# An attention and expert kernel whose row loads keep their place in SyncE's queue

## The chip, the cores and the metric

The kernel runs on one core of a Trainium2 chip. Its engines are TensorE (PE; its weight loads are listed as PEld), VectorE (DVE), ScalarE (ACT), GpSimd (POOL) and SyncE (SP), which here only issues DMAs. Each engine has a queue of its own that it works through in order. The metric is the device time of one execution in microseconds (us).

## What is computed

Causal attention with a decay over 4 batches, 8 heads, 576 positions and 64 columns a head; then a gated feed-forward layer (512 to 2048 to 512); then a soft mixture of 8 experts with 4 slots each. All in float32 in the reference:

```python
scores = scale * np.matmul(q, k.transpose(0, 1, 3, 2))
cum = np.cumsum(np.log(np.clip(f, 0.0001, 1.0)), axis=-1)
scores = np.where(causal, -1e9, scores + cum[..., :, None] - cum[..., None, :])
attn = softmax(scores)                      # over the last axis
x = np.matmul(attn, v)                      # -> (2304, 512)
h = x @ w_in
x = (h * (1.0 / (1.0 + np.exp(-1.702 * h)))) @ w_out
logits = x @ phi                            # 32 slots
slot_input = softmax(logits over tokens).T @ x
slot_out[e] = np.maximum(slot_input[e] @ w1[e], 0.0) @ w2[e]   # 8 experts
return softmax(logits over slots) @ slot_out
```

## The kernel before

The attention is cut into 20 rows, numbered 0 to 19: 4 batches of 5 blocks of positions (four of 128, one of 64). A row needs its queries and the keys and values of the rows of its batch up to itself. To keep precision with float16 matmuls, keys, queries and values are split into a high and a low float16 part.

For each row, `load_row` (lines 274 to 293) issues loads of keys, queries and values from DRAM on SyncE (line 290) into the tiles kf, qf and vf, of which there is one buffer each. `prep_row` (295 to 346) then makes the operands of the score matmuls: ScalarE casts the keys (line 300, kbn) and the queries (303, qbn), VectorE copies them beside the decay terms (304, 305 and 310: kan, qan) and subtracts to get the low parts (307, 311; on GpSimd for rows 1 to 4). The four tiles kan, qan, kbn and qbn, one buffer each, are transposed: for rows 0 to 2 on TensorE, from row 3 on by four DMA transposes on SyncE (line 328), traced in the order kan, qan, kbn, qbn. Their outputs qa and qb have two buffers each, those of the keys (kab) six. Values are split on ScalarE and VectorE (334, 335). At its end `prep_row` of row r calls `load_row` of row r + 1, so the loads of a row are traced right after the last transpose of the row ahead.

Rows 0 to 4 use a form in which the row maxima are found first (`emit_max`, line 369, tile mt). Rows 5 to 19 use `emit_qk`: score matmuls (533, 534; 545 and 548 for the short rows), the row's exponentials on ScalarE (560), a split into pn (568, 569) and a DMA transpose of pn to ph on SyncE (573), of which ph has three buffers; then the matmuls with the values (610 to 612) read ph.

Beside the attention runs the feed-forward layer (`moe_steps`, lines 754 to 779: matmuls hp, 762 to 764), in 9 pieces of 256 tokens, and ahead of it the conversion of its weights (lines 203 to 262: tiles raw, low, w, wo), which come as 32 loads of 512 KB on SyncE. Attention and feed-forward steps are traced interleaved. After both, 128 loads of 256 KB bring the expert weights.

What order the instructions get is not that of the trace: the tile framework sorts each engine's queue on a simulated time line when the kernel is built, and lets an instruction pass another on its engine where no data or buffer stands against it. `tc.keep_in_program_order(x)` adds one edge, from the instruction traced last on x's engine to x, so that x cannot be sorted ahead of that one. In the kernel before it is used for the first key cast and for some filler matmuls.

Of the kernel before, what the change touches and what calls it, by code (L numbers as in the profile page):

```python
# [30 lines left out]
def attention_moe_softmoe(ctx, tc, q, k, v, f, w_in, w_out, phi, w1, w2, out):  # L31
    nc = tc.nc
# [93 lines left out]
    def setup_decay():  # L126
        fs = ap_.tile([BH, S], F32, tag="kab2", name="fs")
        nc.sync.dma_start(out=fs, in_=f.rearrange("b h s -> (b h) s"))

        nc.gpsimd.memset(nmst, 1.0)  # L130
        nc.scalar.activation(out=nmst, in_=nmst, func=AF.Ln)
        ones = ap_.tile([BH, S], F32, tag="kab3", name="ones")
        nc.vector.memset(ones, 1.0)
        cum = ap_.tile([BH, 128 * NQ], F32, tag="kab4", name="cum")
        nc.vector.memset(cum[:, S:], 0.0)
        load_row(0, "kq")
        nc.vector.tensor_scalar(
            out=fs, in0=fs, scalar1=1e-4, scalar2=1.0, op0=ALU.max, op1=ALU.min
        )
        nc.scalar.activation(out=fs, in_=fs, func=AF.Ln)  # L140
        r = ap_.tile([128, NQ, BH], F32, tag="dg", name="cres")
        nc.scalar.activation(out=r[0:BH, 0, 0:1], in_=fs[:, 0:1], func=AF.Exp)
        nc.vector.tensor_tensor_scan(
            out=cum[:, 0:S], data0=ones, data1=fs, initial=0.0, op0=ALU.mult, op1=ALU.add
        )
        pt = ps_mi("cumT")
        ct = pt[:, 0:NQ * BH].rearrange("p (i c) -> p i c", i=NQ)
        for i in range(NQ):
            nc.tensor.transpose(ct[:, i, :], cum[:, 128 * i:128 * (i + 1)], ident[0:BH, 0:BH])
        nc.vector.tensor_scalar(out=r, in0=ct, scalar1=-1.0 / SC, scalar2=None, op0=ALU.mult)  # L150
        for j in range(3):
            nc.vector.tensor_copy(cpart[:, :, :, j], r)
            if j < 2:
                nc.vector.tensor_tensor(out=r, in0=r, in1=cpart[:, :, :, j], op=ALU.subtract)
# [119 lines left out]
    def load_row(r, names="kqv"):  # L274
        b, i = rows[r]
        n = rows_of[i]
        for nm in names:
            if nm == "v" and b in B32:
                VV[r] = t = ap_.tile([128, H, D + 1], F32, tag="vv", name="vv", bufs=6)
                nc.gpsimd.memset(t[0:n, :, D:D + 1], 1.0 / VS)  # L280
                t = t[:, :, 0:D]
            elif r < 3:

                if r not in first_kq:
                    first_kq[r] = wp.tile([128, 2, 512], F32, tag=f"o{7 - r}", name="kqf")
                t = first_kq[r][:, nm == "q"].rearrange("p (h d) -> p h d", h=H)
            else:
                t = ap_.tile([128, H, D], F32, tag=nm + "f", name=nm + "f", bufs=1)
            src = {"q": q, "k": k, "v": v}[nm]
            nc.sync.dma_start(  # L290
                out=t[0:n], in_=src[b, :, 128 * i:128 * i + n, :].rearrange("h p d -> p h d")
            )
            nat[r, nm + "f"] = t

    def prep_row(r):
# [46 lines left out]
        if r == 0:  # L342
            load_row(0, "v")
            load_row(1, "v")
        elif r + 1 < len(rows):
            load_row(r + 1)
# [875 lines left out]
```

## Time and profile before

| | |
|---|---|
| median of 3 runs | 600.77 us (592.6 to 602.49) |
| profiled execution | 600.44 us |
| its span, first to last instruction | 598.7 us |
| busy: PE, DVE, ACT, POOL | 531.8, 357.7, 311.0, 69.8 us |
| mean granted TensorE clock | 0.938 of full speed |
| row loads (keys, queries, values) | 256 KB each (128 KB for the short rows), about 4 us to landing |

All times of the profile are from one execution and count from its first instruction. A busy engine need not be the one that sets the time; a wait is listed as "who waited, for whom". A DMA's own line shows how long SyncE took to issue it, not when its data landed.

### The profile page before, as it was taken

The numbers are of one execution on the slowest core, as the hardware profiler recorded it, in microseconds if no ns is written. First come the engines' busy times: TensorE is split into PE (matmuls) and PEld (weight loads), VectorE is DVE, ScalarE is ACT, GpSimd is POOL, SyncE is SP. The second block draws the span as 40 slices with busy tenths as digits, with TensorE's granted clock in tenths as the row PEclk, the third lists the DMA queues.
The fourth block names the chain that finished last, engine by engine and source line by source line (L and its number), as shares of the span: only waits on it lengthen the run. The fifth ranks groups of instructions, "written<-read, shape, count | busy, mean of one in ns | idle before, by whom it ended". The sixth has DMA issues, their size and how long they took to land.

```text
span 598.7 us, 13680 instructions
## 1 busy us (share of the span) xinstructions
PE 531.8 (89%) x5399; PEld 337.0 (56%) x5399; DVE 357.7 (60%) x956; ACT 311.0 (52%) x602; POOL 69.8 (12%) x120
## 2 busy tenths in 40 slices
PE   4484899999989999999989989989999989899992
PEld 4473668867756656655556555565665544374331
DVE  8978769646765476695585666785653332320242
ACT  6756577647765465665566655765542332201122
POOL 4866443310000000000000000000000000000000
PEclk9677699989998999999999999998997999869997
DMA  9996494959994374999964799954551399929988
GB/s 250 265 346 159 96 203 144 213 106 176 170 179 76 54 134 79 177 162 167 149 102 92 129 165 190 159 74 90 79 78 24 116 371 384 338 92 338 380 282 267
DMA packets 229823, 105.63 MB, mean 176 GB/s; under 512 B 202592, under 2 KB 211296, under 8 KB 229760
## 3 DMA queue, kind: packets, MB, share of 16 engines
q1 hardware_dynamic: 227296, 102.41, 74.9%
q10 hardware_dynamic: 2464, 2.36, 1.2%
q8 instruction: 42, 0.69, 0.5%
q14 instruction: 21, 0.17, 0.1%
HBM read 64.63 MB, written 4.72 MB: 116 GB/s over the span
## 4 chain that ended last, share of the span: by engine, by line
PE 67%; DMA 11%; DVE 7%; ACT 6%; issue 3%; POOL 2%; SPq 1%; ACTq 1%; POOLq 0%; DVEq 0%
PE hp L762 9%; PE hp L763 8%; PE hp L764 8%; PE gT L738 5%; DMA kf<-in_k_dram 3%; DMA ph<-pn 3%; PE p L742 3%; PE pv L605 3%; PE sp L862 3%; PE pv L610 3%; PE l L1102 3%; DMA qb<-qbn 2%; PE so L1125 2%; PE wps L252 2%; PE scs L533 2%
## 5 line engine op out<-in xcount | busy, mean ns | idle before, releaser
L762 PE MATMUL hp<-w,xt 128*128 128x512 f16 x288 | 111.0, 385 | 0.0
L763 PE MATMUL hp<-w,xt 128*128 128x512 f16 x288 | 110.5, 384 | 0.0
L764 PE MATMUL hp<-w,xt 128*128 128x512 f16 x288 | 110.1, 382 | 0.0
L560 ACT ACTIVATE pf<-scs,mx 128x512 f32<-128x512 f32 (+3 forms) x108 | 58.1, 544 | 39.9 <-DVE mx L556 32.7
L771 DVE SCALAR_TENSOR_TENSOR g<-g,hp 128x512 f32<-128x512 f32 x72 | 49.2, 683 | 45.5 <-ACT g L770 45.4
L770 ACT ACTIVATE g<-hp 128x512 f32<-128x512 f32 x72 | 42.6, 592 | 62.0 <-PE hp L764 61.7
L569 DVE SCALAR_TENSOR_TENSOR pn<-pf,pn 128x512 f16<-128x512 f32 (+2 forms) x78 | 51.1, 657 | 27.7 <-ACT pn L568 26.7
L568 ACT ACTIVATE pn<-pf 128x512 f16<-128x512 f32 (+2 forms) x78 | 47.2, 608 | 21.4 <-DMA ph<-pn 20.3
L556 DVE CUSTOM_DVE_ANT_0 scs<-scs,zmq 128x256 f32<-128x256 f32 (+3 forms) x96 | 46.9, 498 | 13.8 <-PE scs L534 11.3
L610 PE MATMUL pv<-vv,ph 128*128 128x65 f16 (+2 forms) x360 | 48.3, 200 | 6.8 <-DMA ph<-pn 4.8
L738 PE MATMUL gT<-ident,g 128*128 128x128 f32 x288 | 47.7, 287 | 1.3 <-DVE g L771 1.2
L611 PE MATMUL pv<-vv,ph 128*128 128x65 f16 (+2 forms) x360 | 48.0, 197 | 0.0
L612 PE MATMUL pv<-vv,ph 128*128 128x65 f16 (+2 forms) x360 | 47.7, 196 | 0.0
L740 ACT COPY gt<-gT 128x512 f32<-128x512 f32 x72 | 41.5, 582 | 11.5 <-PE gT L738 11.2
L762 PEld LDWEIGHTS <-xt 128*128 128x128 f16 x288 | 29.1, 101 | 32.6 <-issue 10.4
L764 PEld LDWEIGHTS <-xt 128*128 128x128 f16 x288 | 28.5, 99 | 33.1 <-issue 2.0
L610 PEld LDWEIGHTS <-ph 128*128 128x128 f16 (+2 forms) x360 | 35.1, 103 | 18.0 <-issue 8.0
L763 PEld LDWEIGHTS <-xt 128*128 128x128 f16 x288 | 28.4, 99 | 23.0 <-issue 1.6
L738 PEld LDWEIGHTS gT<-ident,g 128*128 128x128 f32 x288 | 33.2, 144 | 11.9 <-issue 4.6
L611 PEld LDWEIGHTS <-ph 128*128 128x128 f16 (+2 forms) x360 | 35.6, 104 | 3.4 <-issue 1.0
L533 PE MATMUL scs<-kab,qa 128*128 128x128 f16 x240 | 34.0, 221 | 3.3 <-ACT pf L560 3.3
L612 PEld LDWEIGHTS <-ph 128*128 128x128 f16 (+2 forms) x360 | 35.7, 104 | 1.0 <-issue 0.4
(215 smaller groups left out, 1043.3 us busy)
## 6 DMA issues: line engine op xcount, KB each, us to landing
we<-in_moe_w_dram SPq DMA_DIRECT2D x128, 256.0 KB, 5.4
raw<-in_moe_w_in_dram SPq DMA_DIRECT2D x16, 512.0 KB, 7.4
raw<-in_moe_w_out_dram SPq DMA_DIRECT2D x16, 512.0 KB, 5.5
kf<-in_k_dram SPq DMA_DIRECT2D x13, 256.0 KB, 4.0
qf<-in_q_dram SPq DMA_DIRECT2D x13, 256.0 KB, 3.7
vf<-in_v_dram SPq DMA_DIRECT2D x12, 256.0 KB, 3.9
out_dram<-ob SPq DMA_DIRECT2D x8, 256.0 KB, 3.2
out_dram<-ob ACTq DMA_DIRECT2D x8, 256.0 KB, 4.0
```

Of the source, the lines that this page charges most:

```text
L556: nc.vector.tensor_tensor_reduce(out=o, in0=o, in1=mask, scale=-SC, scalar=3.0e38 if n == 128 else DG[r][1][:, u], op0=ALU.add, op1=ALU.mi ...
L560: nc.scalar.activation(out=pf[:, hh * nb:(hh + 1) * nb], in_=o, func=AF.Exp, bias=mx[:, hh:hh + 1], scale=-1.0)
L568: nc.scalar.activation(out=pn[:, 0, 0:w], in_=pf, func=AF.Copy, scale=PB)
L569: nc.vector.scalar_tensor_tensor(out=pn[:, 1, 0:w], in0=pf, scalar=PB, in1=pn[:, 0, 0:w], op0=ALU.mult, op1=ALU.subtract)
L610: nc.tensor.matmul(o, lhsT=ph[0:rr, 0, off:off + n], rhs=vh, start=(j == 0), stop=False)
L611: nc.tensor.matmul(o, lhsT=ph[0:rr, 0, off:off + n], rhs=vl, start=False, stop=False)
L612: nc.tensor.matmul(o, lhsT=ph[0:rr, 1, off:off + n], rhs=vh, start=False, stop=(j == i))
L738: nc.tensor.transpose(pt[:, a * 128:(a + 1) * 128], g[:, a * 128:(a + 1) * 128], ident)
L762: first = nc.tensor.matmul(hp, lhsT=xt[:, 0, kk, ts], rhs=win(0, fg, kk), start=(kk == 0), stop=False)
L763: nc.tensor.matmul(hp, lhsT=xt[:, 0, kk, ts], rhs=win(1, fg, kk), start=False, stop=False)
L764: nc.tensor.matmul(hp, lhsT=xt[:, 1, kk, ts], rhs=win(0, fg, kk), start=False, stop=(kk == KD - 1))
L771: nc.vector.scalar_tensor_tensor(out=g, in0=g, scalar=1.0, in1=hp, op0=ALU.add, op1=ALU.mult)
```

## The change

Loads of row 4 and later get `keep_in_program_order`. The edge of a key load goes to the transpose of qbn of the row ahead, that of a query load to the key load of its row, that of a value load to the query load.

```diff
             src = {"q": q, "k": k, "v": v}[nm]
-            nc.sync.dma_start(
+            moved = nc.sync.dma_start(
                 out=t[0:n], in_=src[b, :, 128 * i:128 * i + n, :].rearrange("h p d -> p h d")
             )
+            if r > 3:
+                tc.keep_in_program_order(moved)
             nat[r, nm + "f"] = t
```

## Rows read from the trace of the kernel before

**Rows 1.** The page: busy us, share of the span and instructions of each engine.

```profile
PE 531.8 (89%) x5399; PEld 337.0 (56%) x5399; DVE 357.7 (60%) x956; ACT 311.0 (52%) x602; POOL 69.8 (12%) x120
```

**Rows 2.** Busy time by stretch: stretch, its us, engines, granted clock, DMA share, GB/s.

```profile
62.00:105.00 43.00, 41.55 (x377) 32.44 (x377) 33.95 (x67) 29.66 (x54) 18.50 (x18) 0.90 0.65 154
105.00:150.00 45.00, 44.10 (x438) 33.25 (x436) 26.74 (x73) 27.65 (x55) 7.17 (x15) 0.96 0.85 165
150.00:410.00 260.00, 242.73 (x2665) 152.56 (x2665) 176.58 (x526) 157.48 (x320) 2.73 (x26) 0.99 0.78 132
...
53.80:70.90 17.10, 8.73 (x47) 6.84 (x47) 14.41 (x21) 7.85 (x15) 10.70 (x8) 0.50 0.31 76
...
200.00:250.00 50.00, 48.78 (x594) 30.14 (x592) 33.09 (x92) 28.40 (x59) 0.82 (x4) 1.00 0.66 112
350.00:400.00 50.00, 45.81 (x499) 28.10 (x498) 35.92 (x119) 30.93 (x68) 0.46 (x8) 1.00 0.92 150
```

**Rows 3.** The chain that ended last, 62 to 105 us: start, us, what.

```profile
64.11 4.90 DMA kf<-in_k_dram
...
79.91 5.95 DMA qb<-qbn
```

**Rows 4.** Waits from 62 to 410 us: who waited for whom: us, times, longest.

```profile
ACT kbn L300 <- DMA kf<-in_k_dram: 16.0, 9, 4.6
...
ACT qbn L303 <- DMA qb<-qbn: 11.5, 9, 3.1
...
PE pv L610 <- DMA ph<-pn: 4.8, 6, 1.4
```

**Rows 5.** Waits of SyncE's queue, 62 to 410 us.

```profile
SPq L573 <- DVE pn L569: 46.1, 33, 5.3
...
SPq L290 <- DVE qbn L311: 11.4, 7, 4.2
```

**Rows 6.** DMA issues by line: count, KB each, median us to landing.

```profile
kf<-in_k_dram SPq DMA_DIRECT2D x13, 256.0 KB, 4.0
...
qb<-qbn SPq DMA_TRANSPOSE x17, 3.6
```

**Rows 7.** Time line of SyncE's queue: start, us to issue, line, operation, tiles.

```profile
25.08 0.61 SPq L290 DMA_DIRECT2D vf<-in_v_dram  x1
...
45.37 0.60 SPq L290 DMA_DIRECT2D kf<-in_k_dram  x1
...
48.89 1.26 SPq L328 DMA_TRANSPOSE qb<-qbn  x1
...
175.85 0.37 SPq L290 DMA_DIRECT2D kf<-in_k_dram  x1
...
219.79 0.37 SPq L290 DMA_DIRECT2D qf<-in_q_dram  x1
...
245.95 1.47 SPq L328 DMA_TRANSPOSE qb<-qbn  x1
...
254.08 1.26 SPq L328 DMA_TRANSPOSE qb<-qbn  x1
...
351.89 1.29 SPq L328 DMA_TRANSPOSE qb<-qbn  x1
...
359.75 1.23 SPq L328 DMA_TRANSPOSE qb<-qbn  x1
```

**Rows 8.** Time line of PE: the first score matmul of row 12.

```profile
275.48 0.22 PE L533 MATMUL scs<-kab,qa 128*128 128x128 f16 x1
```

**Rows 9.** Time lines of VectorE, GpSimd and PE; idle before and its end in brackets.

```profile
40.08 0.68 DVE L335 SCALAR_TENSOR_TENSOR vv<-vf,vv 128x512 f16<-128x512 f32 x1
...
57.99 1.59 POOL L307 TENSOR_TENSOR kbn<-kf,kbn 64x512 f16<-64x512 f32 x1
...
58.61 2.63 DVE L216 SCALAR_TENSOR_TENSOR w<-w,low 128x512 uint32<-128x512 uint32 x1
...
62.17 0.26 PE L449 MATMUL scs<-qa,kab 128*128 128x128 f16 x1 [10.17 <-DVE mt L369]
```

## Prediction

> **What bounds the kernel now.** I read five views in this order. First the page's busy shares [rows 1]: TensorE (PE) is busy for 89% of the span, the next engine for 60%. That is an average, so second the busy time by stretch [rows 2]. From 62 to 105 us PE has work in 41.55 of 43 us, and from 105 to 410 us, which holds rows 5 to 19 of the attention mixed with the first expert layer, in 44.10 + 242.73 = 286.83 of 305 us. PE's order is fixed when the kernel is built, so what the change can give back there is at most PE's idle time: 1.45 us in the first stretch and 18.2 us in the second. Before 62 us PE is idle about half of the time, but only the loads of rows 4 to 6 reach into that.
>
> Third, the chain that ended last [rows 3]: between 62 and 105 us it runs through the key load of row 5 (4.90 us) and the last transpose of row 4 (5.95 us). A reader may take these 10.9 us for a price; they are not, since PE had other work beside them for all but 1.45 us. Fourth, the waits of the engines [rows 4]: ScalarE stands 16.0 us (9 times) for key loads, and 11.5 us (9 times) for the last transpose of the row ahead, which still reads the buffer qbn that the cast is to write. PE itself waits for the transposed probabilities ph only 4.8 us in all. Fifth, SyncE's queue [rows 5, 7]: it mostly waits for VectorE to make the next pn (46.1 us), which is no loss; 11.4 us it waits with a load at its head whose buffer is not yet read out.
>
> **What the change moves.** No instruction is added or removed. Each key load of rows 4 to 19 gets an order edge to the instruction traced before it on SyncE, the transpose of qbn of the row ahead; its query load gets one to the key load, its value load one to the query load: 48 loads. Only these edges are new; the expert's weight loads and the ph transposes are still sorted as the scheduler likes.
>
> Where do they stand now? I numbered loads and transposes by counting along the queue [rows 7]. Row 4's keys go at 45.37, before row 3's last transpose at 48.89; row 5's values at 25.08, some 55 us before row 4's last transpose at 79.91 [rows 3]; row 12's keys at 175.85 and queries at 219.79, where row 11's last transpose is at 245.95. After the change all of them follow that transpose.
>
> **Price of the later loads.** A transpose holds the queue about 1.3 us, two loads issue in about 0.6 us each, and a load lands 4.0 us after its issue [rows 6, 7]. So row r+1's keys are there about 1.3 + 4.0 = 5.3 us after row r's last transpose is issued and its queries about 0.6 us later. The query cast could not start before that transpose landed anyway, 3.6 us after issue [rows 6]; it loses about 2 us. The key cast loses more, as it could run long before. From one row's last transpose to the next row's, the shortest distances now are 254.08 - 245.95 = 8.1 us (rows 11 to 12) and 359.75 - 351.89 = 7.9 us (rows 16 to 17) [rows 7]; with the loads inside it becomes about 5.9 + two casts + four transposes of 1.3 us, some 12 us: an estimate from these rows.
>
> Does anybody notice? Row 12's last transpose lands about 254.08 + 3.6 = 257.7, and PE takes up row 12's scores at 275.48 [rows 8]. 4 us of lateness meet 17 us of cover. For the other rows the last transpose waits for its output buffer (two buffers, so the scores of two rows earlier must be done), and the loads have that whole time. I put this term at 0; its bound is in the slower rival. If the cover were gone, PE would stand at the first score matmul, and the ph transposes behind the late ones would follow.
>
> On the other engines the casts wait as now, only for another thing: the 16.0 us for key loads may grow from 9 rows to 16 (16 x 1.8 = 28 us), while the 11.5 us for the row-ahead transpose go, since the query load lands after it. 28 against 27.5 us: 0.
>
> At this place the Trainium skill speaks against the change: "DMA: Bandwidth & Descriptors", section "Rules for kernel authors", says to issue a DMA early, compute, and wait for it late. The trace has both cases: keys of row 12 are loaded 70 us early, yet ScalarE waits for keys in 9 rows. By the rule alone, with all 16 pairs of loads exposed, the cost would be 16 x 4.0 = 64 us; with the cover that the rows show it is 0, which is what I use.
>
> **What it may give.** (a) The front. Row 5's value split (0.68 us on VectorE at 40.08) and row 4's key split (1.59 us on GpSimd at 57.99) stand ahead of work that PE is waiting for, the maxima of row 3, in the 10.17 us gap that ends at 62.17 [rows 9]. With later loads the scheduler sorts them later. Bounds 0 and 0.68 + 1.59 = 2.3 us; I take 0.7, the split of values alone, because row 4's loads still land (about 54 us) before its casts. (b) 62 to 105 us: casts of row 5 no longer stand unready in front of VectorE's maxima. Bounds 0 and 1.45; I take 0.5. (c) 105 to 410 us: SyncE no longer stands at a load whose buffer is in use (11.4 us), so some ph transposes go earlier. Bounds 0 and PE's whole wait for ph, 4.8 us; I take a third, 1.5, because row transposes and PE's own use of the ph buffers hold the queue as well.
>
> (d) The reordering itself. The scheduler sorts all queues anew around the moved loads, and no row tells which way that falls. I bound it by PE's idle share in the calmest and in the worst stretch: 1.22 of 50 us and 4.19 of 50 us [rows 2]. If all 305 us were like the one, idle would fall from 18.2 to 7.4 us, a gain of 10.8; like the other, it would rise to 25.6, a loss of 7.4. I take 0.
>
> **Sum.** The profiled execution took 600.44 us (span 598.7 and 1.7 around it), 0.3 under the median of 600.77. 600.44 - 0.7 - 0.5 - 1.5 = 597.7 us.
>
> **Rivals.** *No change (600.4 us).* The order in the queue is another, but every load is hidden in both. For it speaks that PE has only 18.2 us idle in the long stretch and waits for ph in six places only; against it, that the loads now do cause waits of other engines.
>
> *Slower: the turn of a batch is exposed (612.4 us).* At rows 6 and 7, 11 and 12, 16 and 17 two rows are prepared back to back, as key buffers come free only when a batch of the attention is through. If the 4 us per row were not covered there, 3 turns x 4 us = 12 us: 600.4 + 12. It decides only once row 12's last transpose is over 17 us late [rows 8], or if the scheduler has put the scores right behind it. For it speaks that the stretch from 350 to 400 us, a turn, has PE's worst share already; against it the cover just counted. This is the form that the skill's rule on early DMAs would take here.
>
> *Faster by over 2%: the front gap closes (585.9 us).* PE stands idle 10.17 us before 62.17, and in the stretch from 53.8 to 70.9 us its granted clock is 0.50, the lower level of 1.2 GHz [rows 2, 9]; it fell while PE stood in that gap. If the maxima come without the gap, 10.2 us are won, and the 8.7 us of PE's work in that stretch take half, 4.35 us: 600.4 - 14.5. For it speaks that casts and splits of rows 4 and 5 stand in just that stretch; against it that most of the gap is the conversion of the expert's weights (VectorE's line 216 alone took 2.63 us at 58.61 [rows 9]), which the change does not touch.
>
> **How the numbers follow.** Forecast 0.45, no change 0.22, slower rival 0.16, faster rival 0.17. Predicted: 597.7. Its own range is 594 to 601. The bounds of (a) to (d) go from 600.4 - 2.3 - 1.45 - 10.8 = 585.9 to 600.4 + 7.4 = 607.8; with 585.5 to 608 only the slower rival, 0.16, is left out. 2% is 12 us, about what a measurement of this kernel tells from no change: faster 0.17, same 0.67, slower 0.16.
>
> **What the profile of the changed kernel would show.** In SyncE's timeline each key load from row 4 on stands behind the qbn transpose of the row ahead, with no wait of a load for VectorE's qbn. ScalarE's waits for qbn's transpose are nearly gone and its waits for key or query loads have grown. PE's idle time from 105 to 410 us is 16 to 19 us. Row 12's last transpose is about 4 us nearer to row 12's first score matmul, and PE does not wait there. The prediction is wrong if PE's waits name the loads or the row transposes with several us, or if the gap before 62 us is much shorter or longer than 10 us.

## The result and the profile after

The changed kernel takes 594.76 us (median of 12 runs, 589.74 to 601.24) against 600.7 us for the kernel before in 12 runs of the same series. The ratio is 0.9919, with a 95% interval of 0.989 to 0.9948: a small gain, some 3 to 7 us. Ratios and their intervals here leave out executions in a slower state of the chip, so they can differ a little from the quotient of the medians. The profiled execution took 596.54 us (span 594.7), against 600.44 us (span 598.7) before. Predicted were 597.7 us, a range of 594 to 601 for the likeliest case, and "within 2%" with 0.67. So the total came as predicted. Its parts did not, and the rest of this document is about them. In the changed kernel all lines from 293 on have numbers higher by two (369 is now 371, 573 is 575, and so on), and where a run adds lines of its own, those behind them move further.

The busy shares of the page answer to [rows 1]: TensorE (PE) 89% as before.

```profile
PE 527.5 (89%) x5399; PEld 337.5 (57%) x5399; DVE 355.2 (60%) x956; ACT 310.5 (52%) x602; POOL 69.3 (12%) x120
```

Busy time by stretch of the changed kernel, to be laid beside [rows 2] (stretch, its us, engines, granted clock, DMA share, GB/s). The second group holds the two stretches of low clock that matter now.

```profile
62.00:105.00 43.00, 41.58 (x434) 32.81 (x432) 34.83 (x68) 30.04 (x55) 17.55 (x19) 1.00 0.69 159
105.00:150.00 45.00, 42.57 (x424) 31.68 (x422) 31.22 (x93) 30.88 (x61) 5.58 (x13) 1.00 0.84 189
150.00:410.00 260.00, 240.47 (x2637) 150.98 (x2636) 170.76 (x506) 152.74 (x309) 2.73 (x26) 0.98 0.79 129
53.80:70.90 17.10, 13.62 (x133) 11.96 (x133) 16.96 (x26) 11.73 (x23) 12.41 (x10) 0.82 0.62 176
...
53.20:60.00 6.80, 3.54 (x25) 3.54 (x25) 6.73 (x9) 4.36 (x9) 5.70 (x5) 0.50 0.59 144
251.20:258.00 6.80, 4.55 (x42) 4.13 (x43) 6.14 (x28) 4.61 (x13) 0.00 (x0) 0.50 0.81 169
```

Two things are to be seen. From 53.8 to 70.9 us PE issued 133 matmuls where it had issued 47 [rows 2], and the low clock there (0.50, the level of 1.2 GHz) lasts 6.8 us instead of 17.1. And from 105 to 410 us PE is now idle 305 - 42.57 - 240.47 = 22.0 us, where it was 18.2: the stretch that I had expected to gain has lost.

PE's time line of the changed kernel (start, us; in brackets the idle time before and what ended it): the end of the front gap of [rows 9], then the turn to the third batch, row 12.

```profile
56.46 0.26 PE L451 MATMUL scs<-qa,kab 128*128 128x128 f16 x1 [5.55 <-DVE mt L371]
...
249.60 0.70 PE L803 MATMUL lg<-l,rsum 128*128 128x256 f32 x2 [2.33 <-DVE l L797]
...
252.40 0.22 PE L612 MATMUL pv<-vv,ph 128*128 128x65 f16 x1 [1.68 <-DVE x L626]
...
254.75 0.26 PE L535 MATMUL scs<-kab,qa 128*128 128x128 f16 x1 [1.05 <-ACT pf L562]
...
271.04 0.22 PE L535 MATMUL scs<-kab,qa 128*128 128x128 f16 x1
```

The gap ahead of row 3's maxima fell from 10.17 us [rows 9] to 5.55 us and ends 5.71 us earlier. The gaps at 249.60 to 254.75 are new: before, the same matmuls have only 0.75 us (at 259.27) and 0.61 us (at 260.66) ahead of them.

**The two traces laid on each other.** A number that I call the lead carries the comparison: how much earlier the changed kernel had issued the same amount of PE work. It rests on one execution of each kernel. It is worked out from all PE rows of two traces, each matmul counted with its usual distance to the next in the trace of before.

| time in the kernel before, us | 50 | 70 | 110 | 130 | 250 | 270 | 410 | end (spans) |
|---|---|---|---|---|---|---|---|---|
| lead of the changed kernel, us | 0.7 | 7.9 | 8.0 | 9.8 | 11.1 | 4.6 | 5.9 | 4.0 |

So 7.2 us are won between 50 and 70 us, another 3 up to 250, 6.5 lost between 250 and 270 (the turn to row 12), 1.3 won up to 410, and 1.9 lost behind it. Of this last piece I read only that the low clock in the tail lasts 17.1 us in the changed kernel (517.4 to 534.5) and 10.2 us before (524.9 to 528.3 and 531.7 to 538.5).

**The front, from 44 to 62 us.** Ahead of row 3's maxima VectorE converts five pieces of the expert's weights, two instructions each (lines 213 and 216). These are the durations of the ten, in us, from VectorE's time lines:

| kernel | start | the ten | sum | maxima start |
|---|---|---|---|---|
| before | 47.95 | 0.69 0.69 0.69 1.48 1.03 1.15 1.12 0.69 1.64 2.63 | 11.8 | 61.45 |
| after | 45.90 | 0.69 0.69 0.69 0.69 1.20 0.68 0.68 0.69 0.69 1.31 | 8.0 | 55.73 |

Of the 5.72 us by which the maxima start earlier, 2.05 are an earlier start and 3.8 are the same ten instructions running shorter. GpSimd's time line of the changed kernel, below, says why. Two first steps of the conversion (line 208) that in the kernel before run at 51.63 and 54.67 us (1.95 and 1.96 us) stand elsewhere: one of them now runs in the hole that GpSimd had after 45 us.

```profile
43.44 3.01 POOL L208 TENSOR_SCALAR w<-raw 128x512 f32<-128x512 f32 x2
49.27 1.16 POOL L262 TENSOR_TENSOR w<-w,w 128x512 f16<-128x512 f32 x1 [2.81 <-ACT w L261]
50.40 1.97 POOL L208 TENSOR_SCALAR wo<-raw 128x512 f32<-128x512 f32 x1
53.56 1.63 POOL L262 TENSOR_TENSOR w<-w,w 128x512 f16<-128x512 f32 x1 [1.19 <-ACT w L261]
```

Each long conversion of the table lies beside such a line: in the changed kernel the 1.20 at 49.78 beside 49.27 and 50.40, the 1.31 at 54.43 beside 53.56. Of the 64 conversions in the trace of before, the 29 with no GpSimd instruction beside them last at most 0.69 us; of the other 35, 17 last over 0.70 us, the longest the 2.63 us of [rows 9]. The Trainium skill, "SBUF — State Buffer", section "SBUF: two separate sides", says that a VectorE operation with two inputs in SBUF and a GpSimd operation that reads SBUF shut each other out for a whole instruction. The rows agree for the long ones, but not every overlap is long: 18 of the 35 last 0.70 us or less, and in the changed kernel a conversion at 51.57 keeps to 0.68 us wholly beside the GpSimd instruction of 50.40.

The earlier start comes over ScalarE: at 38.30 us, where it split row 5's values (line 334, 0.65 us), it now converts a weight (line 210, 0.69 us), which before came at 43.39 between two exponentials. The conversion that the first of the ten needs (lines 210 and 211 on ScalarE) then starts at 44.65, ahead of the third exponential, and not at 46.71 behind it. The second exponential, right ahead of it, comes 0.65 us earlier; the rest of the 2.05 us is the changed order. SyncE issues the weight loads 0.6 to 1.0 us earlier, since two value loads are no longer ahead of them: row 5's at 25.08 [rows 7], and row 4's, the second of the two in this line of SyncE's queue in the kernel before:

```profile
22.99 2.05 SPq L290 DMA_DIRECT2D vv<-in_v_dram  x2
```

In the changed kernel row 4's values go at 49.57, row 5's at 75.5. A last part of the front lies behind the conversions. Before, row 4's copies into kan and qan stand ahead of row 3's maxima and between them; in the changed kernel two maxima run first, back to back. VectorE before, then after:

```profile
61.25 0.28 DVE L304 COPY kan<-kbn 64x512 f16<-64x512 f16 x1
61.45 0.67 DVE L369 TENSOR_REDUCE mt<-scm 128x1 f32<-128x512 f32 x1
62.52 0.83 DVE L310 COPY qan<-qbn 64x512 f16<-64x512 f16 x1 [0.40 <-ACT qbn L303]
63.28 0.67 DVE L369 TENSOR_REDUCE mt<-scm 128x1 f32<-128x512 f32 x1
```

```profile
55.73 1.27 DVE L371 TENSOR_REDUCE mt<-scm 128x1 f32<-128x512 f32 x2
```


**The turn to row 12, from 238 to 255 us.** SyncE's queue in the changed kernel (start, us to issue), to be read beside [rows 7]:

```profile
237.96 1.51 SPq L330 DMA_TRANSPOSE qb<-qbn  x1
239.51 0.58 SPq L290 DMA_DIRECT2D kf<-in_k_dram  x1
240.14 0.64 SPq L290 DMA_DIRECT2D qf<-in_q_dram  x1
...
244.06 1.23 SPq L330 DMA_TRANSPOSE kab<-kan  x1
...
251.51 1.59 SPq L330 DMA_TRANSPOSE qb<-qbn  x1
```

Row 12's keys are loaded at 239.51, right behind row 11's last transpose; before they were there from 175.85 on. VectorE's time line of the same stretch:

```profile
243.74 0.29 DVE L306 COPY kan<-kbn 128x512 f16<-128x512 f16 x1 [2.70 <-ACT kbn L302]
...
249.04 0.19 DVE L307 COPY kan<-cpart 128x24 f16<-128x24 f16 x1 [2.84 <-DMA kab<-kan]
249.13 0.42 DVE L797 TENSOR_SCALAR l<-p 128x256 f32<-128x256 f32 x1
```

The second line is the copy of the decay terms of row **13** into kan, which has one buffer. It stands early in VectorE's queue, and it must wait until row 12's transpose of kan, issued at 244.06, has landed. With late keys this transpose is late, and it lands 5.0 us after its issue, where row 12's took 3.2 us in the kernel before; why it took longer was not followed. So VectorE stands 2.84 us at a copy of 0.19 us, where the same copy waited 0.32 us before. Behind it stands line 797, for which PE waits 2.33 us; the maxima behind it are late too, ScalarE waits 5.3 us for them, and PE 1.68 and 1.05 us more. Then the granted clock is 0.50 for 6.8 us; PE's 4.55 us of work in it could have been done in half the time. Together (2.33 + 1.68 + 1.05) - (0.75 + 0.61) + 4.55/2 = 6.0 us, an estimate from these rows, of the 6.5 that the lead falls.

The waits from 62 to 410 us in the changed kernel (us, times, longest), to be laid beside [rows 4], and one line of SyncE's for [rows 5]:

```profile
ACT pf L562 <- DVE mx L558: 32.8, 27, 5.3
...
ACT kbn L302 <- DMA kf<-in_k_dram: 22.2, 13, 2.3
...
DVE kan L307 <- DMA kab<-kan: 8.2, 7, 2.8
...
PE pv L612 <- DMA ph<-pn: 3.6, 5, 1.5
...
ACT qbn L305 <- DMA qf<-in_q_dram: 2.5, 4, 0.6
...
SPq L575 <- DVE pn L571: 53.2, 29, 5.5
```

The sums would not have shown the place: the decay copy waits 8.2 us in all, less than the 11.7 us before. What counts is whether PE's next work stands behind the wait, as it does here.

### The profile page after: what moved, and what is told of

Its sections match the earlier page's. It is cut to its first block, busy times and chain, and to the rows that moved or that the text cites. A ratio compares the mean times of both kernels' runs of the same rounds, so it can differ in the third digit from the quotient of the medians.

```text
span 594.7 us, 13696 instructions
## 1 busy us (share of the span) xinstructions
PE 527.5 (89%) x5399; PEld 337.5 (57%) x5399; DVE 355.2 (60%) x956; ACT 310.5 (52%) x602; POOL 69.3 (12%) x120
## 3 DMA queue, kind: packets, MB, share of 16 engines
q1 hardware_dynamic: 227296, 102.41, 75.5%
## 4 chain that ended last, share of the span: by engine, by line
PE 62%; DMA 13%; DVE 11%; ACT 7%; issue 3%; SPq 2%; ACTq 1%; DVEq 0%
PE hp L764 8%; PE hp L766 8%; PE hp L765 7%; DMA ph<-pn 6%; PE gT L740 5%; PE p L744 4%; PE sp L864 3%; PE pv L607 3%; PE l L1104 3%; PE pv L612 2%; DMA kf<-in_k_dram 2%; PE so L1127 2%; DVE low L213 2%; PE scs L535 1%; DMA qf<-in_q_dram 1%
## 5 line engine op out<-in xcount | busy, mean ns | idle before, releaser
L764 PE MATMUL hp<-w,xt 128*128 128x512 f16 x288 | 109.7, 381 | 0.0
L765 PE MATMUL hp<-w,xt 128*128 128x512 f16 x288 | 109.3, 379 | 0.0
L766 PE MATMUL hp<-w,xt 128*128 128x512 f16 x288 | 109.2, 379 | 0.0
L773 DVE SCALAR_TENSOR_TENSOR g<-g,hp 128x512 f32<-128x512 f32 x72 | 49.1, 683 | 46.9 <-ACT g L772 46.7
L612 PE MATMUL pv<-vv,ph 128*128 128x65 f16 (+2 forms) x360 | 47.0, 199 | 5.5 <-DMA ph<-pn 3.6
L742 ACT COPY gt<-gT 128x512 f32<-128x512 f32 x72 | 41.7, 584 | 16.0 <-PE gT L740 14.5
L740 PE MATMUL gT<-ident,g 128*128 128x128 f32 x288 | 46.0, 282 | 1.0 <-DVE g L773 1.0
L613 PE MATMUL pv<-vv,ph 128*128 128x65 f16 (+2 forms) x360 | 46.7, 196 | 0.0
L614 PE MATMUL pv<-vv,ph 128*128 128x65 f16 (+2 forms) x360 | 46.3, 195 | 0.0
L612 PEld LDWEIGHTS <-ph 128*128 128x128 f16 (+2 forms) x360 | 34.6, 102 | 15.8 <-issue 6.7
L613 PEld LDWEIGHTS <-ph 128*128 128x128 f16 (+2 forms) x360 | 34.9, 103 | 3.8 <-issue 0.8
L614 PEld LDWEIGHTS <-ph 128*128 128x128 f16 (+2 forms) x360 | 35.1, 103 | 1.3 <-issue 0.8
```

The lines of the kernel that those rows point to most:

```text
L612: nc.tensor.matmul(o, lhsT=ph[0:rr, 0, off:off + n], rhs=vh, start=(j == 0), stop=False)
L613: nc.tensor.matmul(o, lhsT=ph[0:rr, 0, off:off + n], rhs=vl, start=False, stop=False)
L614: nc.tensor.matmul(o, lhsT=ph[0:rr, 1, off:off + n], rhs=vh, start=False, stop=(j == i))
L740: nc.tensor.transpose(pt[:, a * 128:(a + 1) * 128], g[:, a * 128:(a + 1) * 128], ident)
L764: first = nc.tensor.matmul(hp, lhsT=xt[:, 0, kk, ts], rhs=win(0, fg, kk), start=(kk == 0), stop=False)
L765: nc.tensor.matmul(hp, lhsT=xt[:, 0, kk, ts], rhs=win(1, fg, kk), start=False, stop=False)
```

## The experiments

Two theories stood after this. In theory A the front is won by the loads of rows 4 and 5, and row 12 loses part of it at its turn; rivals saw the gain or the loss spread over many rows. The parts were made apart first.

**Rows 4 and 5 alone (e1_rows45), and rows 6 to 19 alone (e2_rows6on).**

```diff
-            if r > 3:
+            if r in (4, 5):
```

```diff
-            if r > 3:
+            if r > 5:
```

> Only the loads of rows 4 and 5 keep their place; those of rows 6 to 19 are free as before. Theory A (the whole gain is made at the front, before 62 us, by the loads of rows 4 and 5; the later pins cost about 5 us at the turn to batch 2): PE's gap before the row-3 maxima is about 5.5 us instead of 10.17, PE's clock is back at full by about 60 us, and the lead of some 8 us is not lost later: 587 to 592 us, ratio to the kernel before about 0.98. Rival B (the gain comes from the pins of all rows, through SyncE's queue from 105 us on): front as in A or not, ratio 0.995 to 1.00.

> Only the loads of rows 6 to 19 keep their place; those of rows 4 and 5 are free as before. Theory A (gain at the front only, later pins cost): PE's gap near 62 us stays about 10 us, its clock stays low until about 71 us, and the turn to batch 2 costs: 601 to 607 us, ratio 1.00 to 1.01. Rival B (the later pins bring the gain): ratio 0.99.

Measured: rows 4 and 5 alone 598.14 us, ratio 0.9957 (0.9913 to 1.0); rows 6 to 19 alone 605.72 us, ratio 1.0118 (1.0051 to 1.0184). The two halves together, as changes of the time, would be -0.4% and +1.2%; the whole change is -0.8%. They do not add up.

With rows 4 and 5 alone the front is as in the changed kernel (gap 5.56 us, lead 7.6 at 70 and 10.2 at 130), as theory A has it. But the time is 6 us above what it expected, since the lead falls to some 3 us at 170. The place in that kernel: its time lines of VectorE and of PE, then a stretch with the busy times, the granted clock third from the end:

```profile
149.96 0.19 DVE L307 COPY kan<-cpart 128x24 f16<-128x24 f16 x1 [1.01 <-DMA kab<-kan]
150.04 0.68 DVE L773 SCALAR_TENSOR_TENSOR g<-g,hp 128x512 f32<-128x512 f32 x1
```

```profile
150.78 0.66 PE L243 MATMUL woT<-ident,wo 128*128 128x128 f32 x4 [1.82 <-DVE g L773]
```

```profile
152.70:163.00 10.30, 10.30 (x56) 7.55 (x56) 4.85 (x12) 5.40 (x11) 0.00 (x0) 0.50 1.19 186
```

It is a decay copy again, that of row 10: it waits 1.01 us for a transpose of kan, PE's work stands behind it, and after a gap of 1.82 us PE works 10.3 us at the low clock, which costs about 5 us more. The loads of rows 9 and 10 have no edge in this kernel, so it does not take one. A second loss of lead, from 6 us at 200 to 1.6 at 230, is not at a decay copy: none lies there, PE waits 1.66 us for ph at 210.12, and 3.4 us of low clock follow. With rows 6 to 19 alone the front is not won (gap 12.53 us), and at the turn to row 12 the lead goes from 4.2 to -2.3, by the same 6.5 us as in the changed kernel. VectorE's time line of that kernel, then PE's:

```profile
255.63 0.19 DVE L307 COPY kan<-cpart 128x24 f16<-128x24 f16 x1 [2.75 <-DMA kab<-kan]
```

```profile
256.18 0.70 PE L803 MATMUL lg<-l,rsum 128*128 128x256 f32 x2 [2.00 <-DVE l L797]
```

**Row 12 left out (e3_not12), and row 12 alone (e12_only12).**

```diff
-            if r > 3:
+            if r > 3 and r != 12:
```

```diff
-            if r > 3:
+            if r == 12:
```

> As the changed kernel, but the loads of row 12 are free. Up to the turn to batch 2 every engine's order is that of the changed kernel. Theory A (row 12's late key load makes its kan transpose land late, the decay copy of row 13 stands at VectorE's head for it, and PE waits behind): the waits of 2.7 to 2.8 us of VectorE's kan copies between 240 and 252 us are gone, PE's gaps of 2.33 and 1.68 us there too, and 4 to 6 us are won on the changed kernel: 588 to 592 us, ratio 0.98. Rival C (the loss there is the turn's own, whoever loads when, or it moves to row 13 or 14): same as the changed kernel, ratio 0.99.

> The kernel before, with only the three loads of row 12 kept in their place. Up to the turn to batch 2 all is as before. Theory A (row 12's late key load stalls VectorE at the turn): from 240 to 270 us PE loses 2 to 6 us against the kernel before: 603 to 606 us, ratio 1.005 to 1.01. Rival C (the stall belongs to the shifted schedule as a whole): ratio 1.00.

Measured: without row 12's edges 590.47 us, ratio 0.9878 (0.9824 to 0.9932); with them alone 601.04 us, ratio 1.0061 (1.002 to 1.0103). By the ratios, taking the three edges of one row out of 48 is worth 0.4% against the changed kernel, some 2.5 us, but the two intervals overlap, and 0.99, which rival C gave, lies inside: the time alone does not decide. Putting those three edges alone costs 0.6%, some 4 us, clear of 1.00 and where theory A put it. The rows decide for the first kernel. Up to 230 us its VectorE and up to 242 us its PE have the order of the changed kernel. At the turn the decay copy does not wait, and line 803 waits 0.27 us for line 797 instead of 2.33 (time lines of VectorE and PE of e3_not12):

```profile
242.54 0.18 DVE L307 COPY kan<-cpart 128x24 f16<-128x24 f16 x1
```

```profile
245.99 0.70 PE L803 MATMUL lg<-l,rsum 128*128 128x256 f32 x2 [0.27 <-DVE l L797]
249.70 0.19 PE L612 MATMUL pv<-vv,ph 128*128 128x65 f16 x1 [2.64 <-DVE x L626]
```

The clock is low for 3.4 us there instead of 6.8, and the lead falls by 3.8 us (12.7 to 8.9) instead of 6.5. So row 12's late loads make about 2.7 us of the loss here; a gap of PE of 2.64 us, for VectorE's line 626, is there without them, and row 12's edges alone lose some 4 us at this turn. The parts do not add up here either.

**The decay copy kept behind.** If the copy's place in VectorE's queue is what costs, the loads can stay late and the copy alone be held in its traced place, behind the copy of the same row's kbn.

```diff
-        nc.vector.tensor_copy(kan[0:n, :, D:D + 3], cpart[0:n, i, b * H:(b + 1) * H, :])
+        dec = nc.vector.tensor_copy(kan[0:n, :, D:D + 3], cpart[0:n, i, b * H:(b + 1) * H, :])
+        if r > 5:
+            tc.keep_in_program_order(dec)
```

> As the changed kernel, and from row 6 on the copy of the decay terms into kan keeps its place behind the copy of the keys into kan, so it no longer stands alone at VectorE's head waiting for the transpose of the row ahead. Theory A (that copy is one of the blockers at the turn): VectorE's waits of kan copies for the transpose of kan, 11.7 us in the kernel before, are nearly gone, PE's gaps at the turn to batch 2 shrink by 2 to 4 us; 591 to 594 us, ratio 0.985. Rival C: the wait goes over to the key copy behind it, no gain, ratio 0.99.

> The kernel before, its loads free, with only the decay copy kept behind the key copy from row 6 on. Theory A (the decay copy blocks VectorE wherever a row's kan transpose lands late; the load pins make it worse only at row 12): front as before (gap about 10 us, lead 0 at 70 us), later some 2 to 5 us won, ratio 0.992 to 0.997. Rival (the copy costs only beside late loads): ratio 1.00. Rival (its order alone makes the gain of the run with both): ratio 0.985.

> The changed kernel with both mends of the turn to batch 2: row 12's loads free, and the decay copy kept behind the key copy from row 6 on. Theory A (both act on the same stall of VectorE there): little more than the better of the two alone, 586 to 589 us, ratio 0.980 to 0.985, PE's gaps between 240 and 255 us under 2 us in all. Rival D (they remove different stalls): both gains add, 582 to 585 us, ratio 0.975.

Measured: on top of the changed kernel (e6_decay_pin) 588.95 us, ratio 0.9841 (0.979 to 0.9893), the ratio that theory A gave, at a somewhat shorter time; on the kernel before, with free loads (e8_decay_alone), 600.77 us, ratio 1.0002 (0.9946 to 1.0057); on the version without row 12's edges (e7_pin_not12) 587.17 us, ratio 0.9814 (0.9746 to 0.9881). So holding the copy back gains nothing on the kernel before, and 0.8%, some 5 us, with the late loads (the two intervals just touch). That does not make it harmless beside free loads: with the edges on rows 4 and 5 alone it cost at row 10, whose loads are free. Time lines of VectorE and PE at the turn in e6_decay_pin, and a stretch behind it with the granted clock third from the end:

```profile
241.01 0.29 DVE L306 COPY kan<-kbn 128x512 f16<-128x512 f16 x1 [2.31 <-ACT kbn L302]
241.22 0.18 DVE L307 COPY kan<-cpart 128x24 f16<-128x24 f16 x1
```

```profile
247.71 0.19 PE L614 MATMUL pv<-vv,ph 128*128 128x65 f16 x1 [2.02 <-DVE x L628]
```

```profile
250.00:258.00 8.00, 8.00 (x77) 4.19 (x74) 7.94 (x30) 7.11 (x18) 0.00 (x0) 1.00 1.20 226
```

Row 12's keys are as late as in the changed kernel, ScalarE's cast too (VectorE waits 2.31 us for it), but no instruction of another row stands waiting for a buffer that is still being read. PE's gaps are 2.02 and 0.61 us, the clock stays up, and the lead falls by 2.4 us (13.8 to 11.4), 4 us less than in the changed kernel. Another 2.7 us of lead were won ahead of the turn, most of them between 150 and 200 us, so not all of the gain belongs to row 13's copy.

What the late keys alone cost cannot be read off this. With row 12's keys early and the copy held (e7_pin_not12) PE's gaps at the turn are only 1.23 and 0.61 us, under the 2 us of theory A, but 6.8 us of low clock follow, and the lead falls by 4 us (16.3 to 12.2). In time this version is where theory A put it, though its interval holds rival D's 0.975 too. It is 1.9%, some 11 us, faster than the kernel before and also beats the changed kernel.

**Which load opens the front.** Each kernel ran once here, so only the rows and differences of several us count. First the values of rows 4 to 6 alone (e9_v456), then the keys and queries of rows 4 and 5 alone (e10_kq45):

```diff
-            if r > 3:
+            if nm == "v" and r in (4, 5, 6):
```

```diff
-            if r > 3:
+            if r in (4, 5) and nm != "v":
```

Third, on the kernel before with all loads free (e11_split5), ScalarE's cast of row 5's values kept in its traced place, so that the values come early and are not split early:

```diff
-            nc.scalar.activation(out=vv[0:n, 0, :, 0:D], in_=vf[0:n], func=AF.Copy, scale=VS)
+            high = nc.scalar.activation(out=vv[0:n, 0, :, 0:D], in_=vf[0:n], func=AF.Copy, scale=VS)
+            if r == 5:
+                tc.keep_in_program_order(high)
```

> Only the value loads of rows 4, 5 and 6 keep their place behind the query load of their row; keys and queries are free as before. Theory E (the front's gain comes from the value work of row 5, which leaves VectorE and ScalarE before 45 us and lets the weight conversion start earlier): PE's gap before the row-3 maxima is 5 to 7 us. Rival F (it comes from the keys and queries of row 4, whose casts and splits stand in the weight conversion's way from 56 to 62 us): gap stays at 10 us or more.

> Only the key and query loads of rows 4 and 5 keep their place; values are free as before. Theory E (value work of row 5): PE's gap before the row-3 maxima stays at 10 us or more. Rival F (keys and queries of row 4 and 5): gap 5 to 7 us, PE's clock back at full by about 62 us.

> The kernel before, all its loads free, with only the cast that begins the value split of row 5 kept in its place on ScalarE (line 334, first time), so that the value load stays at 25 us and only the split leaves the front. Theory E1 (ScalarE's and VectorE's 0.65 and 0.68 us for the split, at 38 and 40 us, delay the weight conversion behind them): PE's gap before the row-3 maxima is 5 to 7 us. Rival E2 (it is the DMA of the values, 256 KB ahead of the weight loads, that delays them): the gap stays at 10 us.

Measured: 593.82 and 606.19 us, with the kernel before at 600.38 in their series, and 602.81 us, with the kernel before at 598.38 in its own. PE's time lines of the three, in this order, have this gap ahead of row 3's maxima:

```profile
57.84 0.26 PE L451 MATMUL scs<-qa,kab 128*128 128x128 f16 x1 [6.68 <-DVE mt L371]
```

```profile
62.59 0.27 PE L451 MATMUL scs<-qa,kab 128*128 128x128 f16 x1 [8.22 <-DVE mt L371]
```

```profile
62.59 0.27 PE L451 MATMUL scs<-qa,kab 128*128 128x128 f16 x1 [11.30 <-DVE mt L371]
```

The values alone bring the conversions of the changed kernel: the ten take 8.0 us and start at 45.86, and the gap is in theory E's range. But they bring only half of the front: the lead at 70 us is 3.8 instead of 7.9. Row 4's keys and queries are early there, and on VectorE their copies still stand ahead of the maxima and between them:

```profile
56.37 0.82 DVE L306 COPY kan<-kbn 64x512 f16<-64x512 f16 x1 [0.57 <-ACT kbn L302]
57.12 0.67 DVE L371 TENSOR_REDUCE mt<-scm 128x1 f32<-128x512 f32 x1
58.26 2.37 DVE L312 COPY qan<-qbn 64x512 f16<-64x512 f16 x1 [0.47 <-ACT qbn L305]
60.55 0.67 DVE L371 TENSOR_REDUCE mt<-scm 128x1 f32<-128x512 f32 x1
```

With keys and queries alone moved, the maxima run back to back, and the ten take 9.7 us, the last of them 0.69 instead of 2.63, as row 4's key split on GpSimd no longer lies beside it; but they start late, and the gap of 8.22 us is neither theory E's 10 nor rival F's 5 to 7. So both have a part: the values set the start and most of the length of the conversions, the keys and queries of row 4 what stands between conversions and maxima.

Moving only the split's compute away does not open the front: the ten take 9.8 us but start at 48.59, and the weight loads have the old order and times. That speaks for the place of the value loads ahead of the weight loads, and not for the 0.68 us of the split; it is one execution, in which ScalarE's order changed elsewhere too, and row 4's values (128 KB, beside the 256 KB of row 5) were never moved without row 5's. What of it acts through the weights' earlier landing and what through their changed order among themselves was not separated. The 606.19 us of keys and queries alone is no clean price: from 42.2 to 49.1 us that execution shows a clock of 0.51 and loses 2.8 us there (below).

**GpSimd beside the conversions.** On the kernel before, the two line-208 steps at 51.63 and 54.67 us are given to ScalarE; VectorE's list up to row 3's maxima stays the same. Then the same edit on the best version.

```diff
-        if n % 2 < 1:
+        if n % 2 < 1 and n not in (10, 18):
             nc.gpsimd.tensor_scalar(out=val, in0=hi.bitcast(F32), scalar1=2.0 ** -111, scalar2=None, op0=ALU.mult)
```

> Edit: the kernel before, loads free; two of the weight conversions' first steps (numbers 10 and 18 of the list, the two that GpSimd runs at 51.63 and 54.67 us in the trace of before, 1.95 and 1.96 us) are given to ScalarE (about 0.65 us each). VectorE's list of instructions up to row 3's maxima is as before. In the trace of before the ten VectorE conversions ahead of these maxima (lines 213 and 216, from 47.95 to 61.17) take 11.8 us in all, in the changed kernel the same ten take 8.0. Theory P: they are stretched by GpSimd working beside them, since none that runs alone lasts over 0.69 us. Then with 3.9 us of GpSimd's work gone they take 8 to 10 us in all, PE's gap ahead of row 3's maxima shrinks from 10.2 to 7 to 9 us, and PE is 1.5 to 3.5 us earlier at 70 us, more if the low clock ends earlier; time 596 to 600. Theory Q: they are long for the state of their inputs (late weight loads), and GpSimd is only beside them: the sum stays at 11 to 12 us, the gap at 10 to 11, the time at 600 to 603.

> Edit: the version with all loads from row 4 on but row 12's in program order and with the decay copies from row 6 on in program order, and the same two first steps given to ScalarE. Theory P: of the ten conversions, 8.0 us in the changed kernel, two still lie beside GpSimd (1.20 and 1.31 us); the rest of the 5.6 us gap ahead of row 3's maxima can fall by at most 1.1 us, and what falls there moves the time by 0.5 to 2 us below that version's 587.2: 585 to 588. Theory Q: nothing changes at the front: 587 to 589. What is re-sorted behind it (batch turns) may cost or give some us in either case, read from the lead at 70 us and at 250 us.

Measured: 598.18 us, ratio 0.9966 (0.9942 to 0.999), and 588.29 us, ratio 0.9772 (0.9722 to 0.9822). On the kernel before the ten conversions take 9.0 us instead of 11.8, with the same loads and the same list on VectorE, and the gap is 8.87 us instead of 10.17 (PE's time line of e13_less_pool):

```profile
63.16 0.27 PE L449 MATMUL scs<-qa,kab 128*128 128x128 f16 x1 [8.87 <-DVE mt L369]
```

Gap, sum and time lie where theory P put them; the lead at 70 us does not (-1.5 instead of +1.5 to 3.5), because this execution too had the low clock from 42 to 49 us and came 2.7 us late to the conversions. So GpSimd beside them is one cause of the long front, worth about 2 us of the time here (0.6 to 3.5 by the interval). On the best version the edit is a miss. In its profiled execution, at 595.59 us the slowest of its five, the front gap becomes 6.75 us instead of 5.55, as the remaining GpSimd steps move up and meet three of VectorE's ten (1.20, 1.50 and 1.64 us), and its time cannot be told from 587.17.

## Why the prediction was right, and where it was not

The total was right because two errors of about 7 us had opposite signs; that is luck. Step by step, as put down:

**(a) The front: 0.7 us taken, bounds 0 and 2.3; the lead at 70 us is 7.9.** The value split did leave VectorE's way: the maxima at 40.69 start at 40.04, 0.65 us. The term missed three things. First, the weight loads behind the values of rows 4 and 5 and what ScalarE and VectorE do with them: 2.05 us of earlier start, with those 0.65 in it. I had counted only row 5's value load; row 4's left the front as well. Second, what stretches VectorE's conversions: 3.8 us. The row was in front of me: a conversion of 2.63 us beside a GpSimd instruction in [rows 9], where the same instruction alone lasts 0.69. I took its duration as fixed. Third, the clock: it came back at 60.0 instead of 70.9, and PE's work at the low level went from 8.73 to 3.54 us, (8.73 - 3.54)/2 = 2.6 us. The key split and the copies of row 4, which I left at nothing because its loads still land before its casts, are part of this too: with the values alone moved the lead stays at 3.8. The faster rival named the place, and the clock, but let the argument against it win: "the conversion of the expert's weights, which the change does not touch". No weight instruction was edited; their loads and their neighbours were moved. About half of that rival's 14.5 us came true.

**The price of the later loads: 0 taken; it was 6.5 at one turn.** The cover that I counted held. Row 12's last transpose is issued at 251.51 and landed 3.8 us later (that line's median in the changed kernel), and row 12's first score matmul is at 271.04, without a wait: 15.7 us of cover, where it was 17.8. From row 11's last transpose to row 12's it now takes 251.51 - 237.96 = 13.6 us, where my estimate was some 12. So the slower rival's deciding point, lateness over 17 us at the scores, was never reached, and yet PE lost time. The step that failed is the sentence that PE would stand at the first score matmul if anywhere. I had listed what waits for the transpose as a reader, and not what waits for it as the next writer of its input: the decay copy of the row after, which the scheduler had put early in VectorE's queue, with the expert's and the attention's work behind it. Keeping that copy back takes 4 us of the 6.5 away at this turn and 0.8% off the time; leaving row 12's loads early takes 2.7 us away there and 0.4% off the time, the latter not clear of noise.

Against the rule of the Trainium skill that I weighed ("DMA: Bandwidth & Descriptors", section "Rules for kernel authors"), my 0 came out too low and the rule's 64 far too high. It holds at row 12. At rows 4 and 5 it is turned round: value loads, row 5's issued 50 us earlier than the changed kernel does it without missing them, stood ahead of loads that were needed sooner.

**(b) 62 to 105 us: 0.5 taken; 0.1 there.** The lead goes from 7.9 at 70 to 8.0 at 110. PE's busy time of the stretch is the same, 41.58 of 43 us, at a clock of 1.00 instead of 0.90; that gain belongs to (a), and a bound by PE's idle time alone, as I took it, could not contain it.

**(c) and (d), 105 to 410 us: +1.5 and 0 taken; the lead falls from 8.0 to 5.9, -2.1.** SyncE no longer waits with a load for VectorE's qbn, as foreseen, and PE's waits for ph fell from 4.8 to 3.6 us, about the 1.5 taken. Idle time of PE rose to 22.0 us, out of the 16 to 19 given: the turn to row 12 took 3 to 4 us of it. The rest of the re-sorting was kind: the lead rises by 3.1 us between 110 and 250.

**The signs given.** Key loads stand behind the qbn transpose of the row ahead: right. ScalarE's waits: 11.5 us for that transpose gone, 16.0 for keys became 22.2 and 2.5 for queries; 24.7 against the 28 foreseen (16 x 1.8 is 28.8). PE does not wait at row 12's scores: right; by the medians the last transpose is 2.1 us nearer to them, not 4. "Wrong if the gap before 62 us is much shorter than 10 us": it is 5.55, and that sign did show that the sum had the wrong parts.

**What stays open.** Why rows 4 and 5 alone lose their lead at 150 us while the whole change doesn't is read from rows (the same copy) but not tried, and their loss at 210 us was not followed. Some 4 us are lost at the turn to row 12 even with row 12's loads early, with the copy free and with it held; what causes them was not tried. The 1.9 us of the tail were not followed. How weight order and weight time share the earlier start, and row 4's values and row 5's, was not separated.

## What to carry to other kernels

When a transfer is made later, list not only who reads its data but who may write its buffer next, and look at what stands behind that writer on its in-order engine: there the price appeared, with all readers covered by 16 us. When a transfer is taken from the front of a queue, price what moves up behind it, and ask of every long instruction in the stretch whether it is long by itself or by its neighbour. A sum that comes out right is not yet an explanation; here +8 and -6.5 us stood in place of three small gains, and holding back one copy of 0.2 us a row, with one row's loads left early, made 0.8% into 1.9%.

## What the runs showed of the hardware

A VectorE conversion with two inputs, 128x512, lasted at most 0.69 us where no GpSimd instruction ran and up to 2.63 us beside GpSimd, where about half of them (18 of 35) kept to 0.70 us; taking 3.9 us of GpSimd's work out of the stretch shortened ten of them from 11.8 to 9.0 us.

A gap of PE was often followed by a granted clock of 0.50, and the time at that level was not in proportion to the gap: 6.8 us after the 5.55 us gap, 13.7 us (54.0 to 67.7) after 6.68 us with the values alone, 17.1 us after 10.17 us before, but also 10.3 us after a gap of 1.82 us, 6.8 us after 1.23 and 0.61 us with the copy held and row 12's loads early, and none after 2.02 and 0.61 us with the copy held alone. Two of the profiled executions (keys and queries alone; the kernel before with less GpSimd work) had the low level from 42 to 49 us after gaps of 1.1 to 1.2 us at 38.5 and 1.92 us at 41.2; four others passed gaps of 0.5 and 1.9 to 2.0 us at the same places at full clock. That cost 2.7 to 2.8 us of a single execution, so a price read from one profile needs a second look before it is believed.
